# Two row pairs of h of the first pair of chunks, moved from the plain product with w_down to the 2x2 scheme of seven products

## The chip, the cores and the metric

One core of one Trainium2 chip runs the kernel. The time is device microseconds of one execution of the whole program; before is the median of three runs, 595.25 us (594.69 to 595.85). The profile and the trace come from one more execution, taken by the hardware profiler; it took 595.02 us, of which 593.3 us lie between its first and its last instruction (the span).

## The reference

The kernel computes, for 2048 tokens of width 512, a gated mix of a linear-attention block and a bilinear feed-forward block (all in float32):

```python
g = sigmoid((x * gate_w).sum(-1, keepdims=True))
# A: q, k, v = x @ wqkv in 32 heads of 16; phi(t) = where(t > 0, t + 1, exp(t)) + 1e-6
a = ((phi(q) @ kv) / (phi(q) @ z + 1e-6)) @ wo      # kv = phi(k)^T v, z = sum of phi(k)
# B: F = 1792 hidden rows
h = (x @ w_gate) * (x @ w_up)
b = h @ w_down
out = g * a + (1 - g) * b
```

## The kernel before, in words

**Precision.** Every large product is made of three matmuls. A float32 factor is split into a rounded half (`hi`, written by ScalarE, ACT) and the rest (`lo`, a subtraction on VectorE, DVE); the products hi*hi, hi*lo and lo*hi are summed in PSUM. `mm3` issues the three, and each has 128x128 weights and 128x512 data. Six of them, two times three, are called a block of work on TensorE (PE) below.

**Stages.** A first stage builds phi(k), the sums over the tokens and the gates. Then come 32 units, `unit(n)`, numbered 0 to 31: 16 for the first pair of 512-token chunks (pair 0), 16 for the second. In each half, 14 units make one 128-row of h (f0 to f13) for both chunks, and two (`q` units: 6 and 11, then 17 and 21) make 256 rows of q for the attention. A unit is a 2x2 scheme of seven products, each one block of six matmuls, in the order Y, X, Y, R, X, R, S by the PSUM bank written. Between them stand operations that a later product needs: ACT copies bank Y to `m`, DVE writes `bR<-bX,m` (needed by the first product into R), DVE forms `t<-bR,cross` and `bS<-t,bX` (needed by the last product, S). The unit's `cross` tiles become its two blocks of h. During unit n the weights of unit n+1 are split (`wch` on ACT, `wcl` on DVE), and those of n+2 get their sums by an accumulating DMA that GpSimd (POOL) issues (`wr<-in_wgu_add`); SyncE (SP) issues the plain loads.

**Down projection.** h times w_down is summed in eight accumulators `acc` of 128x512 per pair of chunks. In pair 0 all 14 rows go the plain way: `down_jobs` takes two rows at a time and makes eight jobs of six matmuls (`pdn`), and after each DVE adds the bank to its accumulator (`acc<-pdn,acc`). Each row costs splits of its two blocks of h (`hh`, `hl`) and of its 512 columns of w_down (`dh`, `dl`). In pair 1 twelve rows of h and the four rows of the attention go through `seven`: two rows of h by two chunks are a 2x2 block matrix, multiplied with a 2x2 block of w_down in seven products (steps 1, 6, 2, 7, 5, 4, 3). A group has two such row pairs, so fourteen jobs of six matmuls (banks `sa` and `sb`). Step 1 goes into bank a, ACT copies a to b and step 6 goes on in b, and so forth; `ends` holds what is done to the banks after a step. Sums of weight blocks are made by accumulating DMAs from POOL (`w_sum`, tile `ws`), with negated blocks kept in memory (`minus`); sums of blocks of h are made on DVE (`x_sum`).

**Order.** All engines run their own instructions in program order. The program order is written out: `down` emits jobs at four places of each unit, as many as the tables `FIRST` and `SECOND` say; `later` hangs other work on named places of a unit (`PLACES`); `advance` emits the splits, sums and loads of a job of `seven` some jobs ahead (`LEAD_X`, `LEAD_W`), a few per job (`MOST`). A load for the next unit but two is issued at the end of each unit (`w_load`).

Of the kernel before, what the change touches and what calls it, by code (L numbers as in the profile page):

```python
# [14 lines left out]
P = 128  # L15
# [7 lines left out]
NF = F // P  # L23
# [8 lines left out]
LEAD_X = 3  # L32
LEAD_W = 19
GAP_L = 6
GAP_A = 13
HB = 8
XAT = (6, 0, 0, 6, 4, 4, 11, 9, 11, 11, 13, 12)
WUNIT = (4, 3, 2)
FIRST = (
    (1, 1, 2, 3), (0, 2, 0, 2), (1, 1, 0, 1), (1, 1, 1, 0), (0, 2, 1, 2), (0, 1, 1, 3), (0, 0, 1, 0), (0, 0, 3, 0),  # L40
    (2, 0, 1, 3), (1, 1, 1, 1), (1, 0, 3, 1), (0, 2, 1, 1), (2, 0, 3, 3), (0, 0, 0, 3), (2, 1, 0, 0), (3, 1, 3, 3),
)
PLACES = "high low e m c d t s r end".split()
ATT = ((0, 8, 5, 4, 6, 4, 3, -2), (0, 5, 12, 6, 1, 7, 2, 6))
NS = 58
SECOND = (
    (0, 1, 2, 2), (0, 1, 2, 0), (3, 1, 1, 1), (1, 0, 0, 1), (0, 1, 0, 0), (0, 1, 1, 2), (2, 0, 0, 2), (1, 0, 0, 1),
    (1, 1, 1, 2), (3, 2, 2, 0), (1, 0, 1, 1), (1, 3, 0, 2), (0, 3, 1, 0), (2, 1, 0, 2), (2, 2, 1, 3), (3, 2, 1, 1),
)
STARTS = (0, 4, 5, 7)  # L50
MOST = (2, 3, 2, 2)
RELOAD = {1: (1, 1), 5: (4, 4), 6: (6, 6), 7: (7, 7)}
# [12 lines left out]
def gated_mix(ctx: ExitStack, tc, xt, xp, x, wqkv, wq, wq_add, wo, wgu, wgu_add, wdn, gate_w, out):  # L65
# [323 lines left out]
    class Buf:  # L389

        def __init__(self, name, rounded=False):
            self.home = rounded and bool(spare)
            one = spare.pop(0) if self.home else p2.tile([P, CH], F32R if rounded else F32, tag="s", name=name, bufs=NS)
            self.f = one.bitcast(F32) if rounded else one
            self.r = one
            if not self.home:
                live.append(self)
                assert len(live) <= NS
# [23 lines left out]
    def do(n, place):  # L422
        for fn in at.pop((n, place), []):
            fn()
        if n >= units:
            clock[0] += 1
            advance(dve=MOST[0], act=MOST[1])
# [4 lines left out]
    class Job:  # L432

        def __init__(self, mms, chains=(), after=None, apart=False):
            self.mms, self.after, self.apart = mms, after, apart
# [20 lines left out]
    owed, passed = [0], [0, 0]  # L456

    def down(k, all_=False):

        owed[0] += k  # L460
        for _ in range(owed[0]):
            if not jobs or jobs[0].apart and passed[0] == passed[1] and not all_:
                break
# [6 lines left out]
            job = jobs.pop(0)  # L470
            owed[0] -= 1
# [3 lines left out]
            advance(dve=MOST[2], act=MOST[3])  # L475
# [9 lines left out]
    def unit(n, quad=None, sign=None, og=None):  # L485
# [4 lines left out]
        def reload(i):  # L490
            if n + 1 == units and i not in xsum:
                spare.extend(v[:, k] for v in xc[i] for k in range(2))
            elif n + 1 == units:
# [9 lines left out]
                for fn, at_ in zip((high, low), RELOAD[i]):  # L503
# [166 lines left out]

    def minus_store(key, src):
# [3 lines left out]
        dma(minus[key], one.f[:, 0:2 * P])  # L675
        put(one)
# [23 lines left out]
    left = [NF // 2 + 1] * TPP  # L700
# [10 lines left out]
    def down_jobs(pair, group, ends=False):  # L711

        def job(i):
# [18 lines left out]
            def after(pd, o, step):  # L732
                cols = slice(o, o + step)
                if (pair, i) not in acc:
# [20 lines left out]
            return Job(mms)  # L755
# [7 lines left out]
    turn = [0]  # L763

    def seven(pair, pairs, gated=False):

        g = len(pairs)
        chunks = [range(i, min(i + 2, g)) for i in range(0, g, 2)]
        bank, u2, xs, ws, raw, done = {}, {}, {}, {}, {}, set()
        tags = ("dn", "att") if turn[0] % 2 == 0 else ("att", "dn")  # L770
        turn[0] += 1
        first = (pair, 0) not in acc
        if first:
            for i in range(TPP):
                acc[pair, i] = None
# [4 lines left out]
        def block(i, r, dd, sign=1):  # L780
            if sign < 0:
                return pairs[i]["minus"][r]
# [34 lines left out]
        def x_sum(what, i):  # L817
            b = pairs[i]["b"]
            if what == 3:
                b["x"] = Buf("t3")  # L820
                tt(b["x"].f, b[1, 1].f, b[0, 1].f, ALU.add)
            elif what == 1:
                tt(b[0, 1].f, b[0, 1].f, b[0, 0].f, ALU.add)
            elif what == 2:
                tt(b[0, 0].f, b[1, 1].f, b[0, 1].f, ALU.add)
            else:
                tt(b[0, 0].f, b[0, 0].f, b[1, 0].f, ALU.add)
                done.add((what, i))

        OF = {1: (0, 0), 6: (0, 0), 2: (1, 0), 7: "x", 5: (0, 1), 4: (0, 0), 3: (1, 1)}  # L830
# [15 lines left out]
        def to_acc(dd, c, e, src):  # L846
            i = c * KT + dd * 2 + e
            if first:
# [10 lines left out]
        def ends(step):  # L859
            for e in range(2):  # L860
# [11 lines left out]
                elif step == 5:  # L872
                    i = KT + 2 + e
                    if first:
# [11 lines left out]
        def job(step, i):  # L886
# [3 lines left out]
            def mms():  # L890
                if step == 1 and i == 0:
                    for e in range(2):
                        bank["a", e] = psum.tile([P, CH], F32, tag=tags[0], name="sa", bufs=2)
                    for e in range(2):
                        bank["b", e] = psum.tile([P, CH], F32, tag=tags[1], name="sb", bufs=2)
# [10 lines left out]
            def there():  # L906
                return len(pairs[i]["b"]) >= 4
# [3 lines left out]

            chains = [[]]
            if step == 6:
                chains[0] += [("dve", LEAD_X + 4, 1, lambda: x_sum(3, i), there), ("dve", LEAD_X + 3, 1, lambda: x_sum(1, i), always),
                              ("dve", LEAD_X + 2, 1, lambda: x_sum(2, i), after(1, i, "x"))]
            elif step == 4:
                chains[0] += [("dve", LEAD_X + 2, 1, lambda: x_sum(4, i), after(6, i, "x"))]
            chains[0] += [("act", LEAD_X + 1, 1, lambda: x_high(step, i), there), ("dve", LEAD_X, 0, lambda: x_low(step, i), always)]
            if i == chunk[0]:
                get = ("ws", LEAD_W, GAP_A if step == 3 else GAP_L, lambda: w_get(step, chunk),  # L920
                       after(6, chunk) if step == 3 else always)
                adds = [("ws", LEAD_W, GAP_A, lambda of=of: w_sum(step, chunk, *of), always)
                        for of in ((0, 0, -1), (1, 1))]
                chains.append({5: [get, adds[1]], 6: [get, adds[1], adds[0]], 7: [get, adds[0]]}.get(step, [get]))
                chains[1] += [("act", LEAD_X + 2, 1, lambda: w_high(step, chunk), always),
                              ("dve", LEAD_X + 1, 0, lambda: w_low(step, chunk), always)]
            return Job(mms, chains, (lambda: ends(step)) if i == g - 1 else None, step == 6 and i == 0)
# [4 lines left out]
    def attention(pair, j, n):  # L932
# [56 lines left out]
        def norm_high(i):  # L989
# [3 lines left out]
            if pair:  # L993
                if r != c:
                    act(den[i].f, den[i].f, scale=-1.0)
                fps["a", j]["b"][r, c] = den[i]
# [214 lines left out]
```

## Time and profile before

| what | value |
|---|---|
| median of three runs | 595.25 us (594.69 to 595.85) |
| profiled execution / its span | 595.02 / 593.3 us |
| PE busy / weight load busy | 587.9 us (99%) / 483.2 us (81%) |
| DVE / ACT / POOL busy | 476.6 (80%) / 348.5 (59%) / 82.5 us (14%) |
| TensorE clock granted | 1.000 |
| instructions | 7844, of which 2634 matmuls |

Between the span and the time of the same execution lie 1.72 us. A row of the chain of work that ended last gives a start, a length and what ran (`x36`: 36 instructions); rows of the timeline give start and duration of one instruction, in brackets the idle time before it and what ended it. Matmuls overlap, so the distance between their starts tells more than their durations.

### The profile page before, as it was taken

What the parts mean: (1) busy time and instruction counts of PE and PEld (TensorE: products, weight loads), DVE (VectorE), ACT (ScalarE), POOL (GpSimd) and SP (SyncE); (2) the same over time, 40 slices, a digit from 0 to 9 for tenths busy, and PEclk for the clock granted to TensorE, in tenths of its full rate; (3) what the DMA queues carried; (4) which work ended last, traced back from release to release, by engine and by line L of the source; (5) the groups of instructions that cost most, each with busy time, mean ns of one, the idle gap of its engine ahead of it and who ended that gap; (6) DMA issues with size and microseconds to landing.
All of it is one profiled execution on the core that took longest, in us unless ns stands there. A gap on an engine that the chain in (4) does not pass through costs nothing.

```text
span 593.3 us, 7844 instructions
## 1 busy us (share of the span) xinstructions
PE 587.9 (99%) x2634; PEld 483.2 (81%) x2634; DVE 476.6 (80%) x772; ACT 348.5 (59%) x620; POOL 82.5 (14%) x103
## 2 busy tenths in 40 slices
PE   9999999999999999999999999999999999999997
PEld 6888888888888888888888888887788888888886
DVE  6877896675576687775888857997898999699997
ACT  3756674677538445573564646448957846655620
POOL 0011100100011000001110043203204202401000
PEclk9999999999999999999999999999999999999999
DMA  9477946978776968558685878869877957733003
GB/s 291 156 210 130 295 98 209 233 199 239 214 158 169 292 164 233 131 119 182 157 221 139 253 183 220 225 149 236 181 197 141 235 113 172 142 73 62 1 0 142
DMA packets 63064, 103.29 MB, mean 174 GB/s; under 512 B 8288, under 2 KB 33376, under 8 KB 63008
## 3 DMA queue, kind: packets, MB, share of 16 engines
q1 hardware_dynamic: 49568, 68.72, 34.9%
q0 software_dynamic: 13168, 33.56, 33.2%
q10 hardware_dynamic: 288, 0.52, 0.4%
q8 instruction: 20, 0.33, 0.2%
q14 instruction: 20, 0.16, 0.1%
HBM read 86.77 MB, written 16.66 MB: 174 GB/s over the span
## 4 chain that ended last, share of the span: by engine, by line
PE 96%; DMA 2%; ACT 0%; DVE 0%; issue 0%; SPq 0%; DVEq 0%
PE pdn L73 18%; PE bR L73 14%; PE bY L73 14%; PE bX L73 14%; PE pk L73 8%; PE gt L73 7%; PE bS L73 7%; PE sa L73 7%; PE sb L73 6%; DMA rb<-den 1%; DMA wraw<-in_wqkv 1%; PE pw L73 0%; PE pkv L73 0%; DMA den<-den 0%; DVE rb L85 0%
## 5 line engine op out<-in xcount | busy, mean ns | idle before, releaser
L82 DVE TENSOR_TENSOR wcl<-wr,wch 128x512 fp32r<-128x512 f32 (+1 forms) x96 | 73.4, 772 | 1.6 <-ACT wch L79 1.2
L82 DVE TENSOR_TENSOR acc<-pdn,acc 128x512 f32<-128x512 f32 (+1 forms) x71 | 47.4, 680 | 21.4 <-PE pdn L73 21.1
L79 ACT ACTIVATE wch<-wr 128x512 fp32r<-128x512 f32 (+1 forms) x96 | 60.4, 693 | 2.4 <-DMA wr<-in_wgu_add 2.4
L106 POOL DMA_DIRECT2D wr<-in_wgu_add x28 | 27.4, 978 | 233.9 <-ACT wr L79 147.8
L79 ACT ACTIVATE hh<-cross 128x512 fp32r<-128x512 f32 x29 | 18.2, 628 | 50.1 <-DVE cross L82 50.1
L73 PE MATMUL pdn<-hh,dl 128*128 128x512 f32 (+1 forms) x113 | 43.8, 387 | 0.0
L73 PE MATMUL pdn<-hh,dh 128*128 128x512 f32 (+1 forms) x113 | 43.7, 387 | 0.0
L73 PE MATMUL pdn<-hl,dh 128*128 128x512 f32 (+1 forms) x113 | 43.7, 387 | 0.0
L82 DVE TENSOR_TENSOR bR<-bX,m 128x512 f32<-128x512 f32 x32 | 22.3, 696 | 22.9 <-PE bX L73 22.8
L79 ACT ACTIVATE m<-bY 128x512 f32<-128x512 f32 x32 | 19.1, 598 | 36.7 <-PE bY L73 36.4
L79 ACT ACTIVATE cross<-bY 128x512 f32<-128x512 f32 x32 | 19.0, 595 | 34.8 <-PE bY L73 34.7
L79 ACT ACTIVATE wr<-wr 128x512 f32<-128x512 f32 x64 | 36.5, 619 | 2.2 <-DMA wr<-in_wgu 2.2
L73 PE MATMUL bX<-xbl,wch 128*128 128x512 f32 x96 | 37.5, 390 | 0.0
L73 PE MATMUL bX<-xbh,wch 128*128 128x512 f32 x96 | 37.4, 389 | 0.0
L73 PE MATMUL bX<-xbh,wcl 128*128 128x512 f32 x96 | 37.4, 389 | 0.0
L82 DVE TENSOR_TENSOR t<-bR,cross 128x512 f32<-128x512 f32 x32 | 22.0, 687 | 15.3 <-PE bR L73 9.3
L79 ACT ACTIVATE cross<-bX 128x512 f32<-128x512 f32 x32 | 18.9, 590 | 25.3 <-DVE bS L82 25.2
L73 PE MATMUL bR<-xc6h,wch 128*128 128x512 f32 x64 | 25.1, 392 | 0.0
L73 PE MATMUL bR<-xc1h,wch 128*128 128x512 f32 x64 | 25.0, 391 | 0.0
L73 PE MATMUL bS<-xah,wch 128*128 128x512 f32 x64 | 25.0, 391 | 0.0
L73 PE MATMUL bR<-xc1h,wcl 128*128 128x512 f32 x64 | 24.9, 389 | 0.0
L73 PE MATMUL bR<-xc6l,wch 128*128 128x512 f32 x64 | 24.9, 389 | 0.0
(385 smaller groups left out, 1733.7 us busy)
## 6 DMA issues: line engine op xcount, KB each, us to landing
wr<-in_wgu_add POOLq DMA_DIRECT2D x28, 640.0 KB, 7.1
wr<-in_wgu SPq DMA_DIRECT2D x28, 384.0 KB
xraw<-in_x SPq DMA_DIRECT2D x16, 256.0 KB
wdr<-in_wdn SPq DMA_DIRECT2D x16, 256.0 KB
terms<-zq SPq DMA_DIRECT2D x16, 256.0 KB
zt<-terms SPq DMA_DIRECT2D x16, 256.0 KB
rb<-den SPq DMA_DIRECT2D x16, 256.0 KB
ws<-in_wdn SPq DMA_DIRECT2D x30, 128.0 KB
```

The lines of the kernel that those rows point to most:

```text
L73: tc.keep_in_program_order(nc.tensor.matmul(*args, **kw))
L79: pin(nc.scalar.activation(dst, src, func, **kw))
L82: pin(nc.vector.tensor_tensor(dst, a, b, op=op))
L106: tc.keep_in_program_order(nc.gpsimd.dma_start(dst, src, accum_op=ALU.add))
```

## The change

The rows f4 to f7 of pair 0 no longer go the plain way: the row pairs (4,5) and (6,7) form one group of `seven`, whose jobs are queued at the end of unit 4. The negated blocks of these four rows of w_down, which pair 1 also uses, are now made by themselves: `minus_load` and `minus_make` load, negate and store them in units 1 to 4. The block sums of h are formed in another order: of the three that hung on step 6 and waited for all four blocks, one now needs only the first two and one hangs on step 7; a factor is rounded as soon as its own block is there. The tables that place the work are all new.

```diff
+FIRST_SEVEN = (((4, 5), (6, 7)),)
+FIRST_AT = (4,)
+MINUS_AT = (1, 2)
-LEAD_X = 3
-LEAD_W = 19
+LEAD_X = 4
+LEAD_W = 18
-STARTS = (0, 4, 5, 7)
-MOST = (2, 3, 2, 2)
+STARTS = (0, 4, 6, 11)
+MOST = (3, 3, 2, 2)
+MOST_0 = (1, 2, 2, 3)
+LEAD_X0 = 5
+LEADS_0 = (15, 12, 15)
...
+    def minus_load(key):
+        halves[key] = Buf("half")
+        for r, f in enumerate(key):
+            dma(halves[key].f[:, r * 2 * P:(r + 1) * 2 * P], wdn[f][:, 0:2 * P])
+
+    def minus_make(key):
+        one = halves.pop(key)
+        act(one.f, one.f, scale=-1.0)
+        for r, f in enumerate(key):
+            dma(minus[f], one.f[:, r * 2 * P:(r + 1) * 2 * P])
...
-            if what == 3:
-                b["x"] = Buf("t3")
-                tt(b["x"].f, b[1, 1].f, b[0, 1].f, ALU.add)
-            elif what == 1:
-                tt(b[0, 1].f, b[0, 1].f, b[0, 0].f, ALU.add)
+            if what == 1:
+                b["x"] = Buf("t5")
+                tt(b["x"].f, b[0, 1].f, b[0, 0].f, ALU.add)
             elif what == 2:
-                tt(b[0, 0].f, b[1, 1].f, b[0, 1].f, ALU.add)
+                tt(b[0, 0].f, b[1, 1].f, b["x"].f, ALU.add)
+            elif what == 3:
+                tt(b[0, 1].f, b[1, 1].f, b[0, 1].f, ALU.add)
...
-        OF = {1: (0, 0), 6: (0, 0), 2: (1, 0), 7: "x", 5: (0, 1), 4: (0, 0), 3: (1, 1)}
+        OF = {1: (0, 0), 6: (0, 0), 2: (1, 0), 7: (0, 1), 5: "x", 4: (0, 0), 3: (1, 1)}
...
+    for some, n in zip(FIRST_SEVEN, FIRST_AT):
+        later(n, "end", lambda some=some: jobs.extend(seven(0, [fps[0, key] for key in some])))
+    for key, n in zip([key for some in FIRST_SEVEN for key in some], MINUS_AT):
+        later(n, "c", lambda key=key: minus_load(key))
+        later(n + 1, "c", lambda key=key: minus_make(key))
```

On PE the order of the new program is, in units 8 to 10, with [s.i] for the job of step s and row pair i: unit 8: Y X Y R X [1.0] [1.1] R S; unit 9: Y X [6.0] [6.1] [2.0] Y [2.1] [7.0] R X [7.1] [5.0] [5.1] [4.0] R S; unit 10: Y X [4.1] [3.0] [3.1] Y R X R S. Units 8, 9 and 10 have 54, 96 and 60 matmuls; before, each had 66. The program has 2590 matmuls, before 2602 (in the profile's 2634 the 32 small ones into `pkv` count twice).

What stands on DVE in the second half of unit 9 before, from the operation that releases the last products on:

```order
L82 TENSOR_TENSOR t<-bR,cross_2258 128x512
L82 TENSOR_TENSOR wcl<-wr,wch 128x512
L82 TENSOR_TENSOR bS<-t,bX 128x512
L82 TENSOR_TENSOR acc<-pdn,acc 128x512
L82 TENSOR_TENSOR wcl<-wr,wch 128x512
L85 SCALAR_TENSOR_TENSOR rb<-ph,rb 128x512
```

And the same place of the change (`u_2253`, `u_2255` are the two tiles that carry a partial sum from step 6 to step 5, `xl` a factor's second half):

```order
L88 TENSOR_TENSOR t<-bR,cross_2265 128x512
L88 TENSOR_TENSOR wcl<-wr,wch 128x512
L88 TENSOR_TENSOR bS<-t,bX 128x512
L88 TENSOR_TENSOR xl<-cross_2094,xh 128x512
L88 TENSOR_TENSOR u_2253<-sb,u_2253 128x512
L88 TENSOR_TENSOR u_2255<-sb,u_2255 128x512
L88 TENSOR_TENSOR acc<-u_2253,acc 128x512
L88 TENSOR_TENSOR acc<-sa,acc 128x512
```

The two subtractions from bank b, which job [4.0] on PE waits for, stand behind the operations of the unit itself; the additions into `acc` from the plain jobs are gone there.

On DVE in unit 16, the first of pair 1, whose doubled tiles `xc1`, `xb`, `xc6` and `xa` (128x1024) are loaded anew and split, stood before, from `bR` to `bS`:

```order
L82 TENSOR_TENSOR bR<-bX,m_3230 128x512
L82 TENSOR_TENSOR xc1l<-xc1l,xc1h 128x1024
L82 TENSOR_TENSOR xc4l<-cross_3136,xc4l 128x512
L82 TENSOR_TENSOR xbl<-xbl,xbh 128x1024
L82 TENSOR_TENSOR acc<-pdn,acc 128x512
L82 TENSOR_TENSOR t<-bR,cross_3249 128x512
L82 TENSOR_TENSOR wcl<-wr,wch 128x512
L82 TENSOR_TENSOR xc6l<-xc6l,xc6h 128x1024
L82 TENSOR_TENSOR bS<-t,bX 128x512
```

In the change, behind `bR`:

```order
L88 TENSOR_TENSOR xc1l<-xc1l,xc1h 128x1024
L88 TENSOR_TENSOR xc4l<-cross_3187,xc4l 128x512
L91 SCALAR_TENSOR_TENSOR rb<-ph,rb 128x512
L88 TENSOR_TENSOR xbl<-xbl,xbh 128x1024
L88 TENSOR_TENSOR acc<-pdn,acc 128x512 x2
L88 TENSOR_TENSOR ol<-rb,oh 128x512
L88 TENSOR_TENSOR xc6l<-xc6l,xc6h 128x1024
L88 TENSOR_TENSOR acc<-pdn,acc 128x512
L88 TENSOR_TENSOR t<-bR,cross_3313 128x512
L88 TENSOR_TENSOR wcl<-wr,wch 128x512
L88 TENSOR_TENSOR xal<-xal,xah 128x1024
L88 TENSOR_TENSOR bS<-t,bX 128x512
```

Between `bR` and `bS` now stand twelve operations, before seven; PE's order in that unit is Y X pdn pdn Y pdn R X pdn R S, before Y X Y pdn R X and four pdn, R S.

On POOL in unit 18, where pair 0's outputs leave and the weights of the first group of pair 1 get their sums (`ws<-dminus_107`, `ws<-dminus_109` are the second addition for step 6), stood before:

```order
L106 DMA ws<-in_wdn 128x256 x2
L106 DMA wr<-in_wgu_add 128x1280
L749 DMA out<-acc 128x512 x3
L106 DMA ws<-dminus_107 128x256
L106 DMA ws<-dminus_109 128x256
L749 DMA out<-acc 128x512
```

And in the change:

```order
L112 DMA wr<-in_wgu_add 128x1280
L112 DMA ws<-in_wdn 128x256 x2
L775 DMA out<-acc 128x512
L112 DMA ws<-dminus_107 128x256
L112 DMA ws<-dminus_109 128x256
L775 DMA out<-acc 128x512 x2
```

The second addition now stands behind one output instead of three; the rounding of the sum, on ACT, moved from the middle of unit 19 to the last place of unit 18, ahead of unit 19's copy to `m`.

More of the change, by code (lines that the diff above doesn't have):

```diff
@@ L470, in down @@
             job = jobs.pop(0)
+            running[0] = job.group
             owed[0] -= 1
@@ L753, in after @@
                             put(og[pair, c])
-            return Job(mms)
+            return Job(mms, first=not pair)
         return [job((i + TPP // 2) % TPP) for i in range(TPP)]
@@ L769, in seven @@
         bank, u2, xs, ws, raw, done = {}, {}, {}, {}, {}, set()
[L770 to L775, printed above, removed]
+        me = object()
         def half(buf, i):
@@ L904, in mms, with there, sums @@
                     put(*ws.pop((step, chunk)))
[L906 to L907 removed]
+            def there(*some):
+                return lambda: all(one in pairs[i]["b"] for one in some)
             def after(*what):
                 return lambda: what in done
+            def sums(what, lead, ready):
+                return "dve", lead_x + lead, 1, lambda: x_sum(what, i), ready
             chains = [[]]
+            whole = there((1, 1))
             if step == 6:
[L914 to L915 removed]
+                chains[0] += [sums(1, 4, there((0, 0), (0, 1))),
+                              sums(2, 3, lambda: whole() and (1, i, "x") in done)]
+            elif step == 7:
+                chains[0] += [sums(3, 2, lambda: whole() and (1, i) in done)]
```

130 lines of the change are left out of this document (72 added, 58 removed).

## The prediction

> **What bounds the kernel now.** I read the page first, then who waits on PE, then the chain of work that ended last, and last the rows of the engines that feed PE. The page's busy times, the granted clock and the shares of the chain:
>
> ```profile
> span 593.3 us, 7844 instructions
> PE 587.9 (99%) x2634; PEld 483.2 (81%) x2634; DVE 476.6 (80%) x772; ACT 348.5 (59%) x620; POOL 82.5 (14%) x103
> PEclk9999999999999999999999999999999999999999
> PE 96%; DMA 2%; ACT 0%; DVE 0%; issue 0%; SPq 0%; DVEq 0%
> ```
>
> PE is busy throughout, at full clock, and is 96% of the chain. Its waits that the trace could name:
>
> ```profile
> PE warm L73 <- DVE xc1h L129: 1.3, 1, 1.3
> PE sb L73 <- ACT sb L79: 0.2, 1, 0.2
> PE pk L73 <- ACT wkh L79: 0.2, 1, 0.2
> ```
>
> Behind the start only 0.2 us is named. A busy PE need not be a PE at its pace, so I take the pace from pieces of the chain (start, length, what), those at pace first, then the slower ones and the end:
>
> ```profile
> 271.12 8.16 PE pdn L73 x36
> 333.68 1.60 PE bX L73 x6
> 425.57 1.55 PE bR L73 x6
> 427.12 1.65 PE bS L73 x6
> 434.23 1.41 PE bR L73 x6
> 578.54 11.01 PE pdn L73 x54
> 589.58 0.42 DVE acc L82
> ```
>
> 36 matmuls in 8.16 us are 0.2267 us each, a block of six 1.36 us. The slower blocks lose 0.24, 0.19, 0.29 and 0.05 us. One more loss is a gap between two starts in PE's timeline:
>
> ```profile
> 405.63 0.39 PE L73 MATMUL bX<-xbh,wcl 128*128 128x512 f32 x1
> 406.23 0.73 PE L73 MATMUL sb<-xah,xbl 128*128 128x512 f32 x2 [0.20 <-ACT sb L79]
> ```
>
> 0.60 us instead of 0.23 loses 0.37. That makes 1.14 us from 330 us on, nearly all that PE loses there. So the kernel takes as long as PE has matmuls, and every wait that a schedule adds on PE is seen in full.
>
> **What the change removes from PE.** Four rows the plain way are two pairs of rows, eight jobs each, 96 matmuls. As one group they are seven steps by two row pairs, 14 jobs, 84. Twelve fewer at 0.2267 us are **2.72 us**. All stand on the path. The Trainium skill, in "TensorE: Matmul & The Clock Gate", section "Wait — 56ns, not 53.3ns?", gives 215.7 ns from start to start for 512 columns at full clock; by it the twelve would be 2.59 us, an estimate. The row has 226.7 ns, and the measurement decides. The Trainium skill, in "Trainium Kernel Development and Optimization", section "Performance Expectations", calls matmul busy time a bad metric and weight-load busy a good one; by its 81% PE would have room, and fewer matmuls need not shorten anything (a rival below). Here the even starts of the 36 show no room.
>
> **What it adds on the other engines.** These rows price it (count, then busy, mean ns of one):
>
> ```profile
> L82 DVE TENSOR_TENSOR acc<-pdn,acc 128x512 f32<-128x512 f32 x69 | 46.6, 687 | 21.3 <-PE pdn L73 21.1
> L82 DVE TENSOR_TENSOR xl<-cross,xh 128x512 fp32r<-128x512 f32 x12 | 8.1, 684 | 0.6 <-ACT xh L79 0.5
> L82 DVE TENSOR_TENSOR u<-sb,u 128x512 f32<-128x512 f32 x8 | 5.1, 681 | 0.0
> L79 ACT ACTIVATE xh<-cross 128x512 fp32r<-128x512 f32 x12 | 7.5, 629 | 3.3 <-DVE cross L82 3.3
> ```
>
> DVE loses 16 additions, 8 `hl` and 4 `dl` (28) and gets 14 `xl`, 7 `wl`, 8 sums and 12 operations at the steps' ends (41): 13 more. ACT loses 8 `hh`, 4 `dh` and 4 negations (16) and gets 14 `xh`, 7 `wh`, 6 copies and 2 negations (29): 13 more. What one costs in a full queue is the distance of starts:
>
> ```profile
> 540.79 0.68 DVE L82 TENSOR_TENSOR xl<-cross,xh 128x512 fp32r<-128x512 f32 x1
> 541.39 0.68 DVE L82 TENSOR_TENSOR cross<-cross,cross 128x512 f32<-128x512 f32 x1
> 542.00 0.69 DVE L82 TENSOR_TENSOR bR<-bX,m 128x512 f32<-128x512 f32 x1
> 542.60 0.68 DVE L82 TENSOR_TENSOR cross<-cross,cross 128x512 f32<-128x512 f32 x1
> ```
>
> 0.60 us, since operations overlap. 13 are 7.8 us of DVE in a half where it has room:
>
> ```profile
> 93.00:343.00 250.00, 250.00 (x1157) 206.59 (x1156) 186.12 (x289) 145.32 (x262) 24.02 (x28) 1.00 0.75 195
> 343.00:590.00 247.00, 246.33 (x1089) 202.71 (x1087) 216.32 (x346) 145.74 (x261) 51.12 (x61) 1.00 0.62 146
> ```
>
> (the third number on is busy time of PE, PEld, DVE, ACT, POOL). DVE goes from 186 to 194 of 250 us. Hidden as a sum; what counts is the queue in single units. On DMA, SP issues 12 more (12 block loads, 4 half loads, 4 whole loads fewer; the 4 stores of negated blocks stay), POOL 10 more additions; the first stretch has DMA busy 0.75, so that volume is covered. The negated blocks of f4 to f7 move ahead: SP issues their loads in units 1 and 2, past the loads of weights queued there, and ACT negates each a unit later. If such a load were late, ACT's whole queue would wait; a unit has at least 42 matmuls, 9.5 us, and a late load costs its lateness. The early units carry two loads of x fewer, so I take nothing. The sums of blocks of h are as many as before per pair (four), and earlier: nothing.
>
> **Unit 9, step by step.** Units 8 to 10 have 72 DVE operations of 512 columns or so, 43.3 us at 0.60, and 210 matmuls, 47.6 us. Unit 9 alone: 33, with one of 768 columns, 20 us, against 96 matmuls, 21.8 us. From the unit's start: job [4.0] is PE's fourteenth block and starts at 13 x 1.36 = 17.7. It waits for the two `u<-sb,u`, which come after `bR` and nineteen operations behind it. `bR` starts when the second block ends, 2.7 plus 0.2 to 0.3 of delay. Twenty at 0.60 make 12.0; for ACT, whose rounding some of them follow, I count 1.5. So the first subtraction starts at 16.5 and ends at 17.2, the second at 17.8, while [4.0] needs them at 17.7 and 18.4: 0.5 us to spare. Tightest at the unit's head is the second half of the factor of [6.1], ready at 4.2, needed at 4.5. At 0.684 a piece instead of 0.60, if nothing overlapped, the twenty would be 1.7 us later, a wait of 1.2 us, and the 72 would be 49.2 us, 1.6 more than PE. So from nothing to **1.8 us**, and I take 0.1, by the nearest rows (the starts).
>
> **Unit 16.** A wide split takes this distance:
>
> ```profile
> 330.43 1.23 DVE L82 TENSOR_TENSOR xc1l<-xc1l,xc1h 128x1024 fp32r<-128x1024 f32 x1
> 331.57 0.69 DVE L82 TENSOR_TENSOR xc4l<-cross,xc4l 128x512 fp32r<-128x512 f32 x1
> ```
>
> 1.14 us. Between `bR` and `bS` stand four wide and eight narrow: 4.6 + 4.8. With `bR` at 2.9 and 0.6 for itself, `bS` starts at 12.9 and ends at 13.6; product S is the eleventh block and may start at 13.6. No slack: 0 to 0.7 us, I take 0.1. What goes there is the old loss at 333.68, where X waited for `xbl`: that split now comes earlier and its product has two more jobs ahead of it.
>
> **Other old losses.** The gap at 406.23 stood where step 6 follows step 1 with one product between them, while ACT copies bank a to b. In the new order two to four products stand there in every group, so it goes: 0.37. The blocks at 425 to 434 stand in a stretch where all is reordered; they may go (0.53) or come back elsewhere. Together the old 1.14 may all go or all return under other names; I take 0.4 gone net of the terms of 0.1 above, so 0.2 gone in all.
>
> **Sum.** 595.02 - 2.72 - 0.2 = 592.1 for a profiled execution. The median of the runs shown is 0.23 above this one, so **592.3**. The end (the last nine `pdn` jobs, then DVE and the output) keeps its order.
>
> **Rivals.** (1) *DVE takes the bound* in units 8 to 10 or 16, as priced: 592.5 + 1.8 = 594.3. For it: no slack in unit 16. Against: 0.60 between starts. Chance 0.16, of which 0.05 still under 594.1.
>
> (2) *All old losses go and none comes:* 595.25 - 2.72 - 1.14 = 591.4. Chance 0.07.
>
> (3) *The first attention's sums.* Unit 8 is 12 matmuls shorter, and DVE reaches `zt` sooner after `zq`:
>
> ```profile
> L79 ACT ACTIVATE zq<-ph,ezcol,zcol x4: 827/841/848, 190.6 to 192.7; 128x512 f32<-128x512 f32 x4
> L82 DVE TENSOR_TENSOR zt<-zt x2: 683/688/692, 207.8 to 208.6; 128x512 f32<-128x512 f32 x2
> ```
>
> 17.2 us before. Now: unit 7 (60 matmuls, 13.6), less 2.1 into it, where `zq` follows `m`, plus 4.1 into unit 8, where `zt` is the third on DVE behind `bR`; so 15.6. If the data needed all of 17.2, DVE would stand 1.6 us; `bS` has 2.6 us to spare, and behind it the queue of unit 9 takes up the rest: up to 1.6, 594.1. Chance 0.03.
>
> (4) *Slower: a late weight sum stops ACT.* The rounding of step 6's weights now heads ACT's queue ahead of unit 19's `m`, and `bR`, R and S hang on `m`. Before:
>
> ```profile
> 366.14 1.84 POOL L106 DMA_DIRECT2D ws<-dminus  x2
> 379.69 0.62 ACT L79 ACTIVATE xbl<-ws 128x512 fp32r<-128x512 f32 x1
> DMA to landing us min/median/max: 3.1/5.1/11.1
> ```
>
> From the issue's end to its use 11.7 us; now the issue follows the first output, at about 7.7 to 9.5 in unit 18, and the use comes at 84 x 0.2267 = 19.0: 9.5 us. The longest landing of such a sum was 11.1. ACT may be 3.4 us late before R of unit 19 waits (fifth block at 5.4, less `bR`, `m` and the rounding). So PE waits from a landing of 12.9 us, and the gain is eaten with the bound of 0.2% from 12.9 + 2.7 + 1.2 = 16.8. The same holds for the new group's sums ahead of unit 8. Against: nothing landed so late. Price at 18 us: 592.3 + 5.1 = 597.4. Chance 0.08.
>
> (5) *The jobs removed had been filling* and nothing shortens: 595.25. 0.01. That the matmuls aren't removed is excluded: the order has twelve fewer.
>
> **How the numbers follow.** The forecast has 0.65. Faster by over 0.2% (under 594.06; 0.2% is about what a measurement of this kernel can tell from no change): 0.65 + 0.07 + 0.05 = 0.77. Within: 0.11 + 0.03 + 0.01 = 0.15. Slower: 0.08. The range goes from all losses gone less 0.4 for the spread of the runs, 591.0, to rival 1's 594.3.
>
> **What would show it.** Right: twelve fewer matmuls at 0.2267, blocks at 1.36 in units 8 to 10, the gap before `sb` gone. Wrong: a slow block at S of unit 16 or [4.0] (rival 1), DVE waiting for `zt` (3), ACT waiting for `ws` with PE behind it (4). A loss in a stretch that I didn't walk through, units 20 to 31 above all, would make the sum wrong too.

## The result, and the profile after

The changed kernel takes 592.36 us (median of six runs, 591.67 to 594.29), the kernel before in the same comparison 595.23 us (six runs, 594.69 to 595.85). The ratio is 0.9955, with a 95% interval of 0.9941 to 0.997: faster by 0.3 to 0.6%. The forecast was 592.3 us, 2.95 us less than before; measured is 2.87 us less. The profiled execution took 592.41 us.

The page after, with the span, the busy times and the shares of the chain of work that ended last:

```profile
span 590.7 us, 7887 instructions
PE 584.3 (99%) x2622; PEld 480.8 (81%) x2622; DVE 483.8 (82%) x785; ACT 356.0 (60%) x633; POOL 91.2 (15%) x113
PE 92%; issue 3%; DMA 2%; DVE 1%; ACT 1%; POOL 0%; POOLq 0%; ACTq 0%; DVEq 0%
```

PE has twelve matmuls fewer and is 3.6 us less busy, DVE and ACT each 7 us more, about as priced. The mean granted clock is 0.999, before 1.000, and the pace is as it was; from the pieces of the chain after:

```profile
547.08 2.72 PE sb L79 x12
575.64 11.01 PE pdn L79 x54
```

1.36 us for six, and the last nine jobs in 11.01 us, as before. But the waits of PE are others. Behind the start, the trace of after names these on PE (us in total, times, longest):

```profile
PE sb L79 <- ACT xh L85: 0.4, 1, 0.4
PE bR L79 <- DVE t L88: 0.2, 1, 0.2
PE sb L79 <- DVE xl L88: 0.2, 1, 0.2
```

To see them in full, I take **the main stretch**: from the start of the first matmul of unit 0 (into bank Y) to the start of the last matmul of the program. PE's timelines give its two ends, first of the kernel before:

```profile
93.18 0.39 PE L73 MATMUL bY<-xah,wch 128*128 128x512 f32 x1
...
589.26 0.28 PE L73 MATMUL pdn<-xc4h,dh 128*128 128x256 f32 x1
```

and of after:

```profile
92.40 0.39 PE L79 MATMUL bY<-xah,wch 128*128 128x512 f32 x1
...
586.36 0.28 PE L79 MATMUL pdn<-xc4h,dh 128*128 128x256 f32 x1
```

496.08 us became 493.96: 2.12 less, not 2.92. The spans differ by 2.6 us, because what lies ahead of the stretch was 0.78 us shorter in this execution (93.18 to 92.40) and what lies behind it 0.3 us longer (593.3 less 589.26 is 4.04; 590.7 less 586.36 is 4.34). Within the stretch I call every distance between two starts of more than 0.24 us, less the 0.227 of the pace, a **loss**. All of them together are 1.49 us before and 2.14 us after; 0.2 of them, at 108 us, stand in every kernel. Those of before at 334, 406, 425, 427 and 434 us have no successor after; in their place stand three, one each in units 2, 9 and 16.

**Unit 2.** ACT's timeline after: the negation of the blocks of w_down (`half`) stands ahead of the rounding of wo (`woh`). DVE's: `wol` waits for that rounding, with `t` behind it. PE's: the product into R waits for `t`.

```profile
120.91 0.63 ACT L85 ACTIVATE half<-half 128x512 f32<-128x512 f32 x1
121.43 0.63 ACT L85 ACTIVATE woh<-wo_sb 128x512 fp32r<-128x512 f32 x1
```

```profile
122.10 0.69 DVE L88 TENSOR_TENSOR wol<-wo_sb,woh 128x512 fp32r<-128x512 f32 x1 [1.32 <-ACT woh L85]
122.82 0.69 DVE L88 TENSOR_TENSOR t<-bR,cross 128x512 f32<-128x512 f32 x1
```

```profile
122.97 0.39 PE L79 MATMUL pdn<-hl,dh 128*128 128x512 f32 x1
123.57 0.50 PE L79 MATMUL bR<-xc6h,wch 128*128 128x512 f32 x1 [0.20 <-DVE t L88]
123.90 0.39 PE L79 MATMUL bR<-xc6l,wch 128*128 128x512 f32 x1
```

0.60 and 0.33 us instead of 0.23 each lose 0.47.

**Unit 9.** In unit 8 ACT stood for the weight sums of unit 9, and DVE for the sums of the attention:

```profile
200.65 0.62 ACT L85 ACTIVATE wch<-wr 128x512 fp32r<-128x512 f32 x1
204.23 1.37 ACT L85 ACTIVATE wch<-wr 128x512 fp32r<-128x512 f32 x2 [2.96 <-DMA wr<-in_wgu_add]
```

```profile
203.86 0.69 DVE L88 TENSOR_TENSOR zt<-zt 128x512 f32<-128x512 f32 x1 [1.03 <-DMA zt<-terms]
...
208.25 0.69 DVE L91 SCALAR_TENSOR_TENSOR wl<-ws,wh 128x512 fp32r<-128x512 f32 x1
```

From there DVE has no hole up to `xl`, the second half of the factor of job [6.1], and PE waits in that job, first for `xh`, then for `xl`:

```profile
211.92 0.39 PE L79 MATMUL sb<-xl,wh 128*128 128x512 f32 x1
212.72 0.50 PE L79 MATMUL sb<-xh,wh 128*128 128x512 f32 x1 [0.41 <-ACT xh L85]
213.06 0.40 PE L79 MATMUL sb<-xh,wl 128*128 128x512 f32 x1
213.65 0.50 PE L79 MATMUL sb<-xl,wh 128*128 128x512 f32 x1 [0.19 <-DVE xl L88]
213.98 0.40 PE L79 MATMUL sb<-xh,wh 128*128 128x512 f32 x1
```

The four distances 0.80, 0.34, 0.59 and 0.33 lose 1.15 us.

**Unit 16.** DVE ends `bS` at 338.5; PE's timeline shows the product S behind it, 0.40 and 0.31 us after the matmul ahead of each, a loss of 0.25:

```profile
338.24 0.39 PE L79 MATMUL bR<-xc6h,wcl 128*128 128x512 f32 x1
338.64 0.47 PE L79 MATMUL bS<-xah,wch 128*128 128x512 f32 x1
338.95 0.39 PE L79 MATMUL bS<-xal,wch 128*128 128x512 f32 x1
```

### The profile page after: what moved, and what is told of

Same layout as the page of the kernel before. It is cut to its first block, busy times and chain, and to the rows that moved or that the text cites. A ratio compares the mean times of both kernels' runs of the same rounds, so it can differ in the third digit from the quotient of the medians.

```text
span 590.7 us, 7887 instructions
## 1 busy us (share of the span) xinstructions
PE 584.3 (99%) x2622; PEld 480.8 (81%) x2622; DVE 483.8 (82%) x785; ACT 356.0 (60%) x633; POOL 91.2 (15%) x113
## 4 chain that ended last, share of the span: by engine, by line
PE 92%; issue 3%; DMA 2%; DVE 1%; ACT 1%; POOL 0%; POOLq 0%; ACTq 0%; DVEq 0%
PE bR L79 14%; PE pdn L79 14%; PE bY L79 13%; PE bX L79 13%; PE sa L79 9%; PE pk L79 7%; PE gt L79 7%; PE bS L79 7%; PE sb L79 7%; DMA cb<-in_xp 1%; DMA wr<-in_wgu 1%; DMA wraw<-in_wqkv 1%; PE pw L79 0%; PE pkv L79 0%; POOL ws L112 0%
## 5 line engine op out<-in xcount | busy, mean ns | idle before, releaser
L79 PE MATMUL bX<-xbh,wch 128*128 128x512 f32 x128 | 47.3, 390 | 0.0
L88 DVE TENSOR_TENSOR acc<-pdn,acc 128x512 f32<-128x512 f32 (+1 forms) x55 | 36.4, 678 | 12.6 <-PE pdn L79 12.4
L79 PE MATMUL pdn<-hh,dl 128*128 128x512 f32 (+1 forms) x81 | 31.4, 387 | 0.0
L79 PE MATMUL pdn<-hl,dh 128*128 128x512 f32 (+1 forms) x81 | 31.3, 387 | 0.0
L79 PE MATMUL pdn<-hh,dh 128*128 128x512 f32 (+1 forms) x81 | 31.3, 387 | 0.0
L112 POOL DMA_DIRECT2D ws<-dminus x24 | 28.9, 1427 | 11.1 <-DVE wl L88 11.1
L85 ACT ACTIVATE xh<-cross 128x512 fp32r<-128x512 f32 x32 | 19.7, 625 | 14.0 <-DVE cross L88 12.2
L79 PEld LDWEIGHTS bX<-xbh,wch 128*128 128x128 f32 x128 | 24.0, 188 | 5.0
L79 PEld LDWEIGHTS bX<-xbl,wch 128*128 128x128 f32 x128 | 24.0, 188 | 4.9
L112 POOL DMA_DIRECT2D ws<-in_wdn x16 | 22.9, 1878 | 18.1 <-DMA ws<-in_wdn 18.1
```

The lines of the kernel that those rows point to most:

```text
L79: tc.keep_in_program_order(nc.tensor.matmul(*args, **kw))
L85: pin(nc.scalar.activation(dst, src, func, **kw))
L88: pin(nc.vector.tensor_tensor(dst, a, b, op=op))
L112: tc.keep_in_program_order(nc.gpsimd.dma_start(dst, src, accum_op=ALU.add))
```

## The experiments

Twelve runs followed: ten edited kernels, and both kernels once more. The table has the main stretch, all losses in it, and the losses of the change's three places (us; the time is a median where more than one run was made).

| kernel | stretch | all losses | unit 2 | unit 9 | unit 16 | time |
|---|---|---|---|---|---|---|
| before | 496.08 | 1.49 | - | - | - | 595.23 |
| before, profiled again | 496.93 | 2.31 | - | - | - | 595.88 |
| before, twelve matmuls fewer | 494.15 | 2.20 | - | - | - | 592.72 |
| after | 493.96 | 2.14 | 0.47 | 1.15 | 0.25 | 592.36 |
| after, profiled again | 493.78 | 2.03 | 0.48 | 1.04 | 0.25 | 591.96 |
| zt later | 494.21 | 2.44 | 0.47 | 1.28 | 0.25 | 592.44 |
| half later | 492.56 | 0.81 | none | 0.29 | 0.25 | 591.27 |
| wcl behind bS | 493.32 | 1.62 | 0.48 | 0.89 | none | 592.47 |
| weight sums issued first | 493.90 | 2.12 | 0.48 | 0.77 | 0.25 | 592.37 |
| three moves together | 494.23 | 2.43 | none | 1.81 | none | 592.01 |
| x sums later | 497.93 | 6.18 | 0.48 | 4.03 | 0.25 | 596.12 |
| longer unit 8 | 493.31 | 1.56 | 0.48 | 0.44 | 0.25 | 591.48 |
| old block sums | 497.54 | 5.74 | 0.48 | 3.36 | 0.25 | 595.98 |
| best | 492.57 | 0.81 | none | 0.42 | none | 591.27 |

**Twelve matmuls fewer, and nothing else.**

```diff
-mm3(pd, ..., j == 0, j == 1, late=1)
+some = (0, 2) if less and not j and i < 6 else range(3)
+mm3(pd, ..., j == 0, j == 1, late=1, part=some)     # less: the jobs of f4 to f7 of pair 0
```

> The kernel before with twelve matmuls left out of the sixteen plain jobs of rows f4 to f7 (in twelve of them the product of the weights' second half with h's first half, for one of the two rows); nothing else is changed. The main stretch runs from the start of the first matmul of unit 0 to the start of the last matmul: 496.08 us before, 493.96 us after the change. Theory: PE is the bound, so each matmul costs its 0.2267 us: main stretch 496.08 - 2.72 = 493.4, time about 592.5. Then the change's own schedule costs 0.6 us more than these twelve matmuls bring. Rival: the jobs had been filling waits, then the stretch stays near 496.1 and the time near 595.2.

Measured: 592.72 us against 595.26, ratio 0.995 (0.9933 to 0.9968). The stretch is 494.15, only 1.93 shorter; but its losses are 0.71 larger than those of the first profile of before. Without losses the stretches are 494.59 and 491.95, 2.64 apart (2.67 with before's second profile). The matmuls cost what the pace says, and rival 5, that the jobs had been filling, falls. So does the reading that the prediction drew from the Trainium skill, "Trainium Kernel Development and Optimization", section "Performance Expectations": with the weight loads busy for 81% there was no room on PE. What comes on top is a loss of 0.54 at 474 us, more than 230 us behind the last of the edited jobs; DVE had waited 1.17 us for a transfer (`rb`) 15 us ahead of it. The second profile of before, further down, shows that such losses come and go.

**The addition of zt later.**

```diff
-ATT = ((0, 8, 5, 4, 6, 4, 5, 3), ...
+ATT = ((0, 8, 6, 3, 6, 4, 5, 3), ...
```

> The changed kernel, with the third addition of the first attention's sums (tile zt) moved behind the second half of the weights at the end of unit 8, so that DVE doesn't stand for its data; PE's order is the same. Theory: the 1.15 us that PE loses at job [6.1] of unit 9 come from DVE's 1.03 us wait for zt, handed on by a DVE queue without a hole: the loss goes to 0 to 0.3 and the main stretch from 493.96 to 492.8 to 493.1. Rival: it comes from the late sums of the next unit's weights (ACT stands 2.96 us for wr in the same unit) or from the number of operations on DVE alone: the loss stays at 0.8 or more, stretch 493.6 or more.

Measured: the loss in unit 9 stays, 1.28 us, and the time too, 592.44 us. DVE didn't wait for `zt` any more; it waited for `wch`, which ACT could round only when the weight sums were there, at 204.21. The theory that `zt` alone is the cause falls.

**The negation later.**

```diff
-later(n + 1, "c", lambda key=key: minus_make(key))
+later(n + 1, "s", lambda key=key: minus_make(key))
```

> The changed kernel, with the negation of the blocks of w_down (tile half, in units 2 and 3) moved on ACT behind the unit's last rounding of wo. Theory: PE's loss of 0.48 us in unit 2 ahead of the product into R comes from that negation, which stands 0.52 us ahead of woh, which DVE needs ahead of t: the loss goes, stretch 493.96 - 0.48 = 493.5. Rival: it comes from the product into the plain bank that stood there in the kernel before and is gone (the wait for woh was there before as well, covered): the loss stays at 0.3 or more.

Measured: the loss in unit 2 is gone. ACT's timeline has `woh` straight behind `cross`, and PE's has 0.23 between the starts:

```profile
120.70 0.59 ACT L85 ACTIVATE cross<-bY 128x512 f32<-128x512 f32 x1
121.18 0.63 ACT L85 ACTIVATE woh<-wo_sb 128x512 fp32r<-128x512 f32 x1
```

```profile
123.24 0.39 PE L79 MATMUL pdn<-hl,dh 128*128 128x512 f32 x1
123.47 0.39 PE L79 MATMUL bR<-xc6h,wch 128*128 128x512 f32 x1
```

The stretch is 1.40 shorter, not 0.48: in this execution unit 9 lost only 0.29. That part wasn't expected and isn't the edit's doing, as the table shows: with the same order in units 8 and 9 the loss there was 0.29, 0.89, 1.04 and 1.15.

**One weight split behind bS in unit 16.**

```diff
-if n:
+if n and n != units:
     w_low(n + 1, 0)
...
 tt(bank["S"], t.f, bank["X"], ALU.subtract)
+if n == units:
+    w_low(n + 1, 0)
```

> The changed kernel, with one split of the next unit's weights (wcl, 512 columns) moved from ahead of bS to behind it, in unit 16 alone. Theory: DVE's queue sets the start of product S there; 0.60 us less ahead of it takes away the whole loss of 0.25 us: stretch 493.7. Rival: bS waits for its product into X or for the split of xa, which S needs anyway: the loss stays.

Measured: in after `bS` started at 337.80, 0.44 us ahead of the last matmul into R (338.24); now it starts at 337.59, 1.04 us ahead of that matmul, and S follows without a loss:

```profile
338.63 0.39 PE L79 MATMUL bR<-xc6h,wcl 128*128 128x512 f32 x1
338.86 0.39 PE L79 MATMUL bS<-xah,wch 128*128 128x512 f32 x1
```

0.60 us less in DVE's queue took the 0.25 us away: DVE's count of operations set the start of S.

**The weight sums of unit 9 issued first.**

```diff
+if n == 7:
+    w_add(n + 2)
 if n:
     w_high(n + 1)
-w_add(n + 2)
+if n != 7:
+    w_add(n + 2)
```

> The changed kernel; in unit 7 alone ACT prepares the weight sums of unit 9 (the copies and negations into wr) ahead of the rounding of unit 8's weights instead of behind it, so that POOL issues their accumulating DMA 1.8 us earlier; PE's order is the same. Theory, formed after moving zt changed nothing: the loss in unit 9 comes from this sum, which landed at 204.23 us where ACT wanted it at 201.3; ACT then gives wh, and with it DVE's wl, 3.4 us after the landing, and everything behind is in a queue without a hole. It should land near 202.4, the loss at job [6.1] fall from 1.15 to 0 to 0.5 us, and the main stretch from 493.96 to 492.8 to 493.4. Rival: the landing is set by the traffic and not by the issue, or by DVE's own count of operations: loss 0.8 or more, stretch 493.6 or more.

Measured: ACT had the sums 2.4 us earlier, at 201.84, and waited 0.17 us instead of 2.96. Yet unit 9 lost 0.77, and unit 7 a new 0.37, where `bS` stood behind the later `wch`. For now DVE waited for `zt` from the first addition on:

```profile
201.10 0.69 DVE L88 TENSOR_TENSOR zt<-zt 128x512 f32<-128x512 f32 x1 [0.59 <-DMA zt<-terms]
202.08 0.69 DVE L88 TENSOR_TENSOR zt<-zt 128x512 f32<-128x512 f32 x1 [0.29 <-DMA zt<-terms]
```

So neither transfer is the cause alone; hastening the one delays the other.

**The three moves together.**

> The changed kernel with the three moves together: the negation of the blocks of w_down behind the roundings of wo, one weight split of unit 16 behind bS, the weight sums of unit 9 prepared first. Theory: the three losses are independent and add up: 0.47 + 0.25 + 0.7 to 1.15 us less, stretch 492.1 to 492.5, and a time 1.5 to 1.9 us under the changed kernel's, about 590.7. Rival: the gained time makes other transfers late, and half of it comes back elsewhere: stretch above 493.

Measured: 592.01 us (591.21 to 592.96), ratio to before 0.9943 (0.9929 to 0.9956), which is not to be told from the changed kernel's. Units 2 and 16 lose nothing, unit 9 loses 1.81 and unit 7 0.36. The rival holds: DVE waited 1.89 us for `zt`.

```profile
202.17 1.42 DVE L88 TENSOR_TENSOR zt<-zt 128x512 f32<-128x512 f32 x2 [1.89 <-DMA zt<-terms]
```

**Both kernels once more.** No edit.

> The kernel before, profiled once more, to see what differs from one execution to the next: I expect the same losses in the main stretch (1.5 us, stretch 496.0 to 496.2), and a start (up to the first matmul of unit 0) that differs by up to 0.5 us from the 93.18 us of the first profile, because the clock rises at another moment. If the start is the same to 0.1 us, the 0.8 us that the changed kernel's start was shorter belong to the change; if it moves, they don't.

> The changed kernel, profiled once more: losses of 0.47 us in unit 2 and 0.25 us in unit 16 as before if they come from the order of the work; in unit 9 anything from 0.3 to 1.3 us if it comes from the landing of a transfer. Start between 92.2 and 93.2 us.

Measured: the start of before is the same to 0.03 us (93.21), the losses are not: 2.31 instead of 1.49 us. The gap at 406 us, 0.47 with its second half, is now 0.90, and DVE waited 1.32 us for `rb` at 463 us, and 0.39 were lost at 477, where the first profile had neither the wait nor the loss. After lost 2.03 us, in the same places as the first time. So between before and after the losses changed from 1.49 and 2.31 to 2.14 and 2.03. That old losses sat at fixed prices was my reading of a single execution.

**Two x sums later.**

```diff
-XAT = (9, 7, 5, 7, 12, 8, ...
+XAT = (9, 10, 5, 10, 12, 8, ...
```

> The changed kernel, with two quarters of the second pair's x sums (tile cb: two loads of 256 KB by SP, two accumulating DMAs of 256 KB by POOL) moved from units 7 and 8 to units 10 and 11; the order on PE is the same, and so is that on DVE. Theory, formed after the earlier issue of the weight sums only made zt late instead: the loss in unit 9 comes from transfers that share a full DMA while units 7 and 8 are short, so 1 MB less there lets both zt and the weight sums land in time: loss at job [6.1] 0 to 0.4 us instead of 1.04 and 1.15, stretch 492.9 to 493.3. Rival: it is the time from issue to use, not the traffic, that is too short: loss 0.8 or more, stretch 493.6 or more.

Measured: 596.12 us, stretch 497.93. SP issued the loads of `zt` 1.1 us later than in after (193.54 for 192.39), since the stores that they wait for had not landed, and DVE waited 3.79 us:

```profile
204.31 0.69 DVE L88 TENSOR_TENSOR zt<-zt 128x512 f32<-128x512 f32 x1 [3.79 <-DMA zt<-terms]
```

The traffic theory falls in this form: 1 MB less in the stretch made nothing land earlier. What this run showed of the clock stands at the end.

**A longer unit 8.**

```diff
 FIRST = (
-    ..., (2, 0, 0, 2), (0, 3, 0, 0),
-    (0, 0, 1, 1), ...
+    ..., (2, 0, 0, 1), (0, 3, 0, 0),
+    (1, 0, 1, 1), ...
```

> The changed kernel, with one plain job of unit 6 handed on, so that unit 8 has one job (1.36 us) ahead of its fourth product; as many matmuls in all. Theory (time from issue to use): zt and the weight sums of unit 9 have 1.36 us more before DVE and ACT want them, of the 1.0 and 3.0 us by which they were late; the loss of 1.04 to 1.15 us in unit 9 falls to 0 to 0.4. Rival (DVE's own count): unit 8 gets two DVE operations more with the job, 1.2 us, so the queue is as late as it was and the loss stays at 0.8 or more.

Measured: nothing waits for a transfer in unit 8. ACT rounds all three parts in one row, where the changed kernel stood for 2.96 us:

```profile
200.47 1.88 ACT L85 ACTIVATE wch<-wr 128x512 fp32r<-128x512 f32 x3
```

Unit 9 loses 0.44 instead of 1.04 and 1.15, a little over the 0.4 expected, and 0.14 come new in unit 7. POOL issued the sums 3.9 us earlier (190.97 for 194.87), so the time from issue to the moment when ACT wants them grew from 6.4 to 10.0 us: more than the 1.36 of the added job. The edit does more than its name says: unit 6 is a job shorter, and in unit 7 the group's roundings stand in another order on ACT, which no longer stands 2.43 us for one of them ahead of the preparation of these sums (the rows of after are shown under "Unit 9" below).

**The old order of the block sums.**

```diff
-chains[0] += [sums(1, 4, there((0, 0), (0, 1))), sums(2, 3, ...)]        # step 6
-chains[0] += [sums(3, 2, ...)]                                            # step 7
+chains[0] += [sums(3, 4, all_), sums(1, 3, all_), sums(2, 2, after(1, i, "x"))]   # step 6
...
-("act", lead_x + 1, 1, lambda: x_high(step, i), there(OF[step]))
+("act", lead_x + 1, 1, lambda: x_high(step, i), all_)
```

> The changed kernel with the old order of the block sums of h (three sums hang on step 6, and a factor is rounded only when all four blocks are there), all tables as in the change. Job [1.1] then waits for the last block of unit 8 and moves to unit 9, behind the old order's sums. By the prediction the new order is worth nothing by itself: stretch within 0.3 us of 493.9. Rival: it is what lets unit 8 have jobs at all; DVE gets three operations more between the last block and step 6 in unit 9, and the loss there grows by 1.2 to 1.8 us, stretch 495 or more.

Measured: 595.98 us, stretch 497.54: with the old sums the group gives nothing. Job [1.1] stands in unit 9, and on DVE a sum of blocks of h stands ahead of its `xl`. Then ACT's copy of bank a to b stands behind two roundings that wait for DVE's next sums, and step 6 on PE waits for that copy. PE's timeline in unit 9:

```profile
209.60 0.39 PE L79 MATMUL sa<-xh,wl 128*128 128x512 f32 x1
211.23 0.50 PE L79 MATMUL sa<-xl,wh 128*128 128x512 f32 x1 [1.23 <-DVE xl L88]
...
213.40 0.39 PE L79 MATMUL bY<-xc4h,wcl 128*128 128x512 f32 x1
215.37 0.50 PE L79 MATMUL sb<-xh,wh 128*128 128x512 f32 x1 [1.58 <-ACT sb L85]
```

The loss grew by 2.2 us, more than the 1.2 to 1.8 expected; and three losses of 0.2 to 0.7 us came in pair 1 (at 420, 426 and 488 us). The tables that place the work were fitted to the new order and stayed as they are, so this is the price of the old order with these tables.

**The best of them together:** negation later, split behind bS, longer unit 8.

> The changed kernel with the three edits that each took a loss away: the negation of the blocks of w_down behind the roundings of wo, one weight split of unit 16 behind bS, and one plain job of unit 6 handed on to unit 8. If they add up: 493.87 us (mean of the changed kernel's two profiles) less 0.47, 0.25 and 0.56, so a main stretch of 492.6 us, and a time 1.0 to 1.5 us under the changed kernel's 592.36, about 591.1. Rival: as with the three moves tried together earlier, the transfers of units 7 and 8 land at other moments and unit 9 takes 1 us or more back: stretch 493.4 or more, time within 0.5 us of the changed kernel's.

Measured: 591.27 us (runs 590.79 to 591.56, expected about 591.1), ratio to before 0.9926 (0.9909 to 0.9943). The stretch is 492.57 where 492.6 was expected: units 2 and 16 lose nothing and unit 9 loses 0.42. All six runs lie under the six of the changed kernel (591.67 to 594.29), which were made in another comparison. That the edits add up rests on the three places, not on the total: the negation moved alone gave the same stretch and the same time in its one run, since unit 9 happened to lose 0.29 there.

## Why the prediction was right, and where it was wrong

**The matmuls: right.** Twelve fewer were priced at 2.72 us. Left out by themselves they gave 2.64 to 2.67; the changed kernel's stretch without losses (491.82 and 491.75) is 2.8 under before's.

**The old losses and the new ones: wrong in size and place.** I took 0.2 us gone in all. In the means of two profiles each, 1.90 became 2.08: 0.2 us more, 0.4 off the forecast. The old places are clean, as I thought they might be, but three new ones cost more than that.

**Unit 16: the mechanism right, the size small.** Zero slack was the count, 0.1 us was taken, 0.25 came in every profile with that order, and moving one operation of 0.60 us removed it. Rival 1, DVE as the bound, is true at this place.

**Unit 9: the failed step.** The step "tightest at the unit's head is the second half of the factor of [6.1], ready at 4.2, needed at 4.5" named the place, and 0.1 us was taken. Rival 3 named the wait for `zt`, gave it up to 1.6 us, and let it be taken up behind. Two things were missed. The 0.3 us of slack at [6.1] and the queue from `zt` to [6.1] are one: take the start of DVE's `wl` from the start of the first matmul of [1.0] (the first `sa` in unit 8).

| kernel | wl behind the first sa | loss at [6.1] | difference |
|---|---|---|---|
| half later | 4.76 | 0.29 | 4.47 |
| best | 4.84 | 0.42 | 4.42 |
| longer unit 8 | 4.84 | 0.44 | 4.40 |
| weight sums first | 5.24 | 0.77 | 4.47 |
| wcl behind | 5.36 | 0.89 | 4.47 |
| after again | 5.51 | 1.04 | 4.47 |
| after | 5.62 | 1.15 | 4.47 |
| zt later | 5.74 | 1.28 | 4.46 |
| three moves | 6.28 | 1.81 | 4.47 |

The rows of after for it: `sa` at 202.63, `wl` at 208.25. In the order of after, each us that `wl` starts behind 4.47 is lost in full: there is no slack behind it, and what the queue was to take up, it can't. And I hadn't looked at the second transfer, the sums of unit 9's weights. In before POOL issued them at 197.13 and ACT used them at 209.15, 12.0 us later; in after they were issued at 194.87, wanted at 201.3, 6.4 us later, and used at 204.23. From the starts of the units (187.99 and 201.59 before, 182.19 and 195.83 after) one sees where the 5.6 us went. Unit 8, which is 12 matmuls shorter, wants them 5.5 us into the unit where it was 7.6. The larger part is on the side of the issue: POOL issues them 12.7 us into unit 7 where it was 9.1. For POOL waits for ACT, which now rounds factors of the new group first and stands for a sum of blocks of h:

```profile
191.12 0.63 ACT L85 ACTIVATE xh<-cross 128x512 fp32r<-128x512 f32 x1 [2.43 <-DVE cross L88]
191.66 1.87 ACT L85 ACTIVATE wch<-wr 128x512 fp32r<-128x512 f32 x3
```

In before `wch` started at 193.89, 5.9 us into unit 7; here it is 9.5. The sums also landed later behind their issue, 9.3 us where it was 6.5 before. My step on DMA ("that volume is covered", from a share of 0.75) asked for bytes where the time from issue to use was the question. The run with the longer unit 8 shows it: with that time at 10 us, ACT's wait is gone. What is left there, 0.44 us, and 0.42 in the best kernel, is lost although no transfer is waited for: DVE's queue has only one hole there, of 0.16 us, between the start of `zt` and the factor of [6.1]. So for a small part rival 1, DVE's own count, is true here too.

**Unit 2: a step that failed.** "If such a load were late, ACT's whole queue would wait ... so I take nothing": the loads were not late. The negation itself, 0.52 us in ACT's queue ahead of `woh`, cost 0.47 us on PE. In before DVE stood 1.28 us for `woh` at the same place, hidden by a plain job between X and R; the new table has none there. I costed the operation as a sum of ACT's room and not at its place.

**The order of the block sums: wrong as a term.** "As many as before per pair, and earlier: nothing." Undone, with the tables as they are, it costs 3.7 us (497.54 for the mean of 493.96 and 493.78), more than the scheme brings. No term of the sum hung on it, but with these tables it is what lets the group stand in units 8 and 9 without losing more than it brings.

**Rival 4 (late weight sum in unit 18): didn't happen.** ACT rounds `wh` at 368.37 without waiting, and stands 5.32 us for PE's bank Y ahead of `m` at 374.32. Five us of cover were there. The mechanism did come, but in another place and with a sum that no rival names: ACT's 2.96 us in unit 8, for the weights of unit 9.

**"The end keeps its order": it does, and yet it takes 0.30 us more.** From the last matmul's start to the end of the span all kernels built on the change take 4.33 to 4.36 us, the three built on before 4.03 or 4.04. The traces put it behind the last packet of the output, which ends 1.62 us ahead of the span's end before and 1.91 after; why the rest takes longer was not tried.

**The sum came out by offsets.** Means of two profiles: stretch 496.5 to 493.87, 2.63 less; end 0.3 more. That is 2.3 us for the change, inside the interval of the runs (1.8 to 3.5 us); the 0.5 us that are missing to the 2.87 are in neither. In the profiles the start was shorter too, by 0.95 us (means 93.20 and 92.25), but that is no part of the change: every engine has the same instructions up to the first matmul of unit 0. The start moves mostly with the moment at which the clock rises. The traces' record of the full clock begins at 7.18 and 7.29 us in the two profiles of before and at 5.38 and 4.89 in those of after; in the kernel before with twelve matmuls fewer it begins at 5.92 (start 92.75), in the other kernels built on the change at 4.09 to 7.01 (starts 92.11 to 93.09). So it is luck that the forecast came within 0.1 us of the median: stretch and end together gained 0.6 us less than the sum had, and what made up for it in the runs was not priced; of that, the traces show only the start moving.

## What to carry to other kernels

When PE is the bound, a shorter unit is also a shorter time from issue to use for every transfer that was timed by units, and every operation put ahead of the issue shortens it too: check each transfer by that time, not by bytes. An operation that an engine has room for can still cost nearly its full length when something on the critical engine's next step stands behind it in the queue, so price it where it is put. One profile of the kernel before doesn't give the size of its losses where they hang on a transfer: here they were 1.5 us in one execution and 2.3 us in the next.

## What the runs showed of the hardware

The clock of TensorE can drop within the program. In the kernel with the x sums later, two matmuls started 2.18 us apart, with PE idle for 1.79 us between them, and soon after the matmuls started 0.43 us apart instead of 0.23, for 3.2 us:

```profile
212.80 0.39 PE L79 MATMUL sb<-xl,wh 128*128 128x512 f32 x1
214.98 0.50 PE L79 MATMUL sb<-xh,wh 128*128 128x512 f32 x1 [1.79 <-ACT xh L85]
...
216.49 0.63 PE L79 MATMUL sb<-xh,wh 128*128 128x512 f32 x1
216.92 0.63 PE L79 MATMUL sb<-xh,wl 128*128 128x512 f32 x1
```

The busy times in that stretch of the same kernel, with the granted clock behind those of the five engines (0.50):

```profile
215.90:219.00 3.10, 3.10 (x7) 2.50 (x8) 3.10 (x6) 1.92 (x4) 0.00 (x0) 0.50 0.41 148
```

Half the clock. About 1.4 us of the 4.03 lost there are its price, an estimate: six distances with 0.20 too much, and a part of the ones at both ends. Two distances of 1.63 and 1.97 us, 4 us apart (the old block sums) and one of 1.46 (three moves) left the clock at 1.00. The Trainium skill, in "TensorE: Matmul & The Clock Gate", section "Why this matters for your kernels", warns of gaps over about 3 us; here the clock dropped behind 2.18 us, in one execution, with two distances of 0.85 and 0.54 us 7 to 9 us ahead. By the same page of the Trainium skill, section "Wait — 56ns, not 53.3ns?", 512 columns take 426.7 ns at the low clock, which these rows show.

The start of the program shows the same clock rising. The first pairs of matmuls into `pk` start 1.00 and 0.85 us apart in before, 0.68 and 0.46 in after, and the record of the full clock begins at 7.18 and at 5.38 us:

```profile
5.01 1.20 PE L73 MATMUL pk<-wkh,xah 128*128 128x512 f32 x2 [0.16 <-ACT wkh L79]
6.01 1.05 PE L73 MATMUL pk<-wkh,xal 128*128 128x512 f32 x2
6.86 0.78 PE L73 MATMUL pk<-wkl,xah 128*128 128x512 f32 x2
```

```profile
5.10 0.84 PE L79 MATMUL pk<-wkh,xah 128*128 128x512 f32 x2 [0.25 <-ACT wkh L85]
5.78 0.63 PE L79 MATMUL pk<-wkh,xal 128*128 128x512 f32 x2
6.24 0.63 PE L79 MATMUL pk<-wkl,xah 128*128 128x512 f32 x2
```

And the landing of one and the same transfer moved from run to run: `zt` and the weight sums by about 1 us (ACT waited 2.3 to 3.0 us and DVE 0 to 1.0 us in the four kernels with the same order around them: after, after again, half later, wcl behind). Which transfers hold them up stays open: less traffic didn't help, an earlier issue of the one made the other later, and only more time between issue and use took the waits away. One order stands out in the traces: in the six executions in which the weight sums were issued ahead of all four loads of `zt` (before twice, twelve fewer, longer unit 8, old block sums, best) they landed 6.2 to 7.7 us after their issue, in the other eight 8.6 to 9.4. No run was made to tell whether that order is the cause.
